# Attention with one ring of four PSUM places, one copy per turned tile and a written order on three engines

## The chip, the cores and the metric

The kernel runs on one core of one Trainium2 chip. The metric is the time of one execution on the device in microseconds (us); of several executions the median counts. A core has TensorE (PE in the profile, with its weight loads as PEld), VectorE (DVE), ScalarE (ACT), GpSimd (POOL) and SyncE (SP), which here issues the DMAs. SBUF is the working memory, PSUM the eight banks that TensorE writes its products to.

## The reference

An attention with a learned bias, then two expert layers; only the attention is touched:

```python
scores = scale * np.matmul(q, k.transpose(0, 1, 3, 2))      # 4 batches, 8 heads, 576 x 64
rel = (pos[:, None] - pos[None, :]).astype(np.float32)
x = (np.log1p(np.abs(rel)) / psi_i)[..., None]
bias = np.maximum(x @ w1 + b1, 0.0) @ w2                     # one 576 x 576 table a head
scores = scores + bias.transpose(2, 0, 1)[None, :, :, :]
scores = scores - np.max(scores, axis=-1, keepdims=True)
attn = np.exp(scores)
attn = attn / (np.sum(attn, axis=-1, keepdims=True) + 1e-09)
out = np.matmul(attn, v)                                     # then moe, then moe2, on 2304 x 512
```

## The kernel before

The bias tables are made first. Then come 16 **pairs** `i` of two heads of one batch, each in nine **tiles** `t` of 128 queries (tile t = 6 takes the last 64 queries of both heads). The expert layers follow; their first weights and inputs are prepared inside the last pairs by hooks.

A tile passes through these steps; the letter is the one that the change gives it:

- **S** (`scores`, L366): six matmuls into a PSUM tile `s` of two banks (twelve for t = 6). q and k are each split into a high and a low part (`split`, L339 and L341 on POOL, four instructions a pair).
- **z** (L376, DVE): bias minus scores and the row's minimum, read from PSUM.
- **e** (L387, ACT): the exponential, with the row's sum.
- **T** (`transposes`, L405): ten transpositions of e into two PSUM tiles `t` of one bank.
- **g** (L414 on ACT for one of them, L416 on DVE for the other): copies of 320 elements a partition into SBUF, the operand of the product with v.

A pair has besides: **P** (`pv`, L429), the product with v in two halves (256 and 320 queries, 20 records each in the trace), issued in two chunks of 12 and 8 records with a score and a transposition between them; **O** (L436), its copy `xo` and the DMA of it to the scratch `xT` (L438); **R** (`sums`, L444 and L445), the inverse of the sums; **Q** (L447, L449), the inverses transposed, copied and stored to `rs`.

PSUM is held by three pools: `a_ps_s` 2 x 2 banks, `a_ps_t` 3 x 1, `a_ps_o` 1: all eight banks. Scores run `LA` = 4 tiles ahead of the transpositions. From pair 1 on the instructions of PE keep the order in which the program issues them (`pin`); on the other engines the scheduler sets the order. SP loads `raw` (q and k of a pair), `v` and, for every fourth pair, the bias rows `nb` two pairs ahead.

Around the last pairs the hooks of the expert layer run on DVE and ACT: `x_sum` (L538) scales the attention's output as it is read back, `w_narrow` (L565, L568, L569) unpacks a weight, `w_split` (L588) makes its high part, `up` (L601) is the first product, with L612 behind it.

Of the kernel before, what the change touches and what calls it, by code (L numbers as in the profile page):

```python
# [68 lines left out]
def bias_phase(tc, ident, W, cpack, lcol, prow, xmain, xtail, att):  # L69
# [3 lines left out]
    with ExitStack() as ctx:  # L73
# [159 lines left out]
        for k in range(1, NG):  # L233
            nc.sync.dma_start(xm_t[:, k], xmain[:, k])
        att.load(0)
        for k in range(NG):
            cs = [c for c in range(3, -1, -1) if k <= NG - 1 - c]
            if k < 5:
                cs.append(4)
            done = 0  # L240
            for n_, c in enumerate(cs):
                unit(k, c)
                if c in (2, 3) and k + c == 8:
                    att.bias_first(3 - c)
# [14 lines left out]
class Attention:  # L259
# [57 lines left out]
    def load(self, i):  # L317
        nc = self.nc
        hp, b = self.pairs[i]
        if b == 0 and hp > 0:  # L320
            self.bias_tile(hp)
            self.bias_rows(hp, 0, 4)
            self.bias_rows(hp, 4, 1)
        raw = self.rp.tile([P, 1792], F32, tag="raw", name=f"raw{i}")
        nc.sync.dma_start(raw, self.qk[hp, b])
        v = self.vp.tile([P, 2, 5, D], F32, tag="v", name=f"v{i}")
        nc.sync.dma_start(v, self.v_l[hp, b])
        self.st[i] = dict(hp=hp, b=b, i=i, raw=raw, v=v)

    def split(self, i, k):  # L330

# [16 lines left out]
    def scores(self, i, t):  # L348
        nc, st = self.nc, self.st[i]
        slot = self.SLOT[t]  # L350
        if slot == 0:
            st["sum"] = self.op.tile([P, 9], F32, tag="sum", name=f"sum{i}")
        s = self.ps_s.tile([P, 2, 512], F32, tag="s", name=f"s{i}_{t}")
        if slot < 4:
            terms = [(P * slot, 0)]
        elif slot == 4:
            terms = [(512, 0), (576, 1)]
        else:
            terms = [(704 + P * (slot - 5), 1)]
# [14 lines left out]
        z = self.zp.tile([P, S], F32, tag="z", name=f"z{i}_{t}")
        m = self.zp.tile([P, 1], F32, tag="m", name=f"m{i}_{t}")
        nc.vector.tensor_tensor_reduce(  # L376
            out=z.rearrange("p (a b) -> p a b", a=2),
            in0=s[:, :, :288],
            in1=self.nb[st["hp"]][:, slot].rearrange("p (a b) -> p a b", a=2),
            scale=-0.125,  # L380
            scalar=3.0e38,
            op0=ALU.add,
            op1=ALU.min,
            accum_out=m,
        )
        e = self.zp.tile([P, S], F32, tag="e", name=f"e{i}_{t}")
        nc.scalar.activation(e, z, AF.Exp, bias=m, scale=-1.0, accum_out=st["sum"][:, slot : slot + 1])  # L387
        st["e", t] = e

    def g_tile(self, st, h, half):  # L390
        if ("g", h, half) not in st:
            st["g", h, half] = self.gp.tile([P, 5, 320], F32, tag="g", name=f"g{st['i']}_{h}_{half}")
        return st["g", h, half]

    def transposes(self, i, t):

        nc, st = self.nc, self.st[i]
        slot = self.SLOT[t]
        e = st.pop(("e", t))
        tp = [self.ps_t.tile([P, 5, 64], F32, tag="t", name=f"t{i}_{t}_{r}") for r in range(2)]  # L400
        for c in range(5):
            for r in range(2):
                q = slice(64 * r, 64 * r + 64)
                k0 = min(P * c, S - P)
                self.pin(i, nc.tensor.transpose(tp[r][:, c], e[q, k0 : k0 + P], self.ident[q, q]))  # L405
        for r in range(2):
            if slot == 4:
                dst = self.g_tile(st, r, 1)[:, :, 256:]
            else:
                n = slot % 5  # L410
                c0 = P * (n % 2) + 64 * r
                dst = self.g_tile(st, slot // 5, n // 2)[:, :, c0 : c0 + 64]
            if r == 0:
                nc.scalar.activation(dst, tp[r], AF.Copy)  # L414
            else:
                nc.vector.tensor_copy(dst, tp[r])  # L416

    def pv(self, i, half, chunks):
        nc, st = self.nc, self.st[i]
        n = 320 if half else 256  # L420
        if chunks[0] == 0:
            st["o"] = self.ps_o.tile([P, 320], F32, tag="o", name=f"o{i}_{half}")
        o = st["o"]
        for c in chunks:
            for h in range(2):
                g = st["g", h, half]
                self.pin(
                    i,
                    nc.tensor.matmul(  # L429
                        o[64 * h : 64 * h + 64, :n], st["v"][:, h, c], g[:, c, :n], start=c == 0, stop=c == 4  # L430
                    ),
                )
        if chunks[-1] < 4:
            return
        xo = self.op.tile([P, 320], F32, tag="xo", name=f"xo{i}_{half}")
        nc.vector.tensor_copy(xo[:, :n], o[:, :n])  # L436
        c0 = st["b"] * S + 256 * half
        nc.sync.dma_start(self.xT[st["hp"], :, c0 : c0 + n], xo[:, :n])  # L438

    def sums(self, i):  # L440
        nc, st = self.nc, self.st[i]
        hp, c0 = st["hp"], st["b"] * S
        r = self.op.tile([P, 9], F32, tag="r", name=f"r{i}")
# [11 lines left out]
    def open(self, ctx):  # L455
        tc = self.tc
        self.zp = ctx.enter_context(tc.tile_pool(name="a_z", bufs=LA + 1, reuse_waits="tile"))
        self.op = ctx.enter_context(tc.tile_pool(name="a_out", bufs=2, reuse_waits="tile"))
        self.gp = ctx.enter_context(tc.tile_pool(name="a_g", bufs=4, reuse_waits="tile"))
        self.ps_s = ctx.enter_context(tc.tile_pool(name="a_ps_s", bufs=2, space=PSUM, reuse_waits="tile"))  # L460
        self.ps_t = ctx.enter_context(tc.tile_pool(name="a_ps_t", bufs=3, space=PSUM, reuse_waits="tile"))
        self.ps_o = ctx.enter_context(tc.tile_pool(name="a_ps_o", bufs=1, space=PSUM, reuse_waits="tile"))
        self.open_set(ctx, 1)

    def run(self, hooks):
        np_ = len(self.pairs)
        steps = [(i, t) for i in range(np_) for t in range(9)]
        pend = []
        for k in range(4):
            self.split(1, k)  # L470
        for i, t in steps[:LA]:
            self.scores(i, t)
        for n, (i, t) in enumerate(steps + [(np_, 0)]):
            if n + LA < len(steps):
                self.scores(*steps[n + LA])
            if i < np_:
                self.transposes(i, t)
            if n:
                i1, t1 = steps[n - 1]
                if t1 == 8:  # L480
                    self.sums(i1)
            if pend:
                pend.pop(0)()
            if n and t1 in self.DONE:
                pend += [lambda i=i1, half=self.DONE[t1], c=c: self.pv(i, half, c) for c in ((0, 1, 2), (3, 4))]
            if t < 4 and 0 < i < np_ - 1:
                self.split(i + 1, t)
            if t == 2 and i + 2 < np_:
                self.load(i + 2)
            for f in hooks.get((i, t), ()):  # L490
                f()
        for f in pend:
            f()


class Moe:
# [734 lines left out]
```

## Time and profile before

| | us |
|---|---|
| runs | 899.84, 907.18, 911.56 |
| median | 907.18 |
| profiled execution, span of the trace | 898.7 |
| its mean granted TensorE clock | 0.953 |
| PE busy in it | 813.7 (91%) |
| DVE busy in it | 604.0 (67%) |
| ACT busy in it | 487.1 (54%) |
| the pairs, from the first z to the end of the last product | 85.9 to 375.3 |

The profile gives the profiled execution's span, 898.7 us, and no other time for it; the median lies 8.5 us above, and the runs lie 11.7 us apart. Busy shares are averages over stages with different limits, so the rows are read by pair: pair `i` is the time from its first z to that of the next pair.

### The profile page before, as it was taken

How to read it: one execution, taken by the hardware profiler on the slowest of the kernel's cores; microseconds unless marked ns; L12 is line 12 of the kernel's file. 1: busy time of each engine (PE TensorE's matmuls, PEld its weight loads, DVE VectorE, ACT ScalarE, POOL GpSimd, SP SyncE). 2: the span in 40 equal slices, each digit the busy share in tenths (PEclk: the TensorE clock that was granted, in tenths of full speed). 3: DMA queues.
4: the chain of work that ended last, by engine and by line, in shares of the span. 5: the costliest groups of instructions: out<-in, count | busy, mean ns of one | idle time of the engine just before them, and what ended most of it. 6: DMA issues, size and time to landing. Idle time of an engine off the chain costs nothing.

```text
span 898.7 us, 18451 instructions
## 1 busy us (share of the span) xinstructions
PE 813.7 (91%) x7428; PEld 655.7 (73%) x7428; DVE 604.0 (67%) x1085; ACT 487.1 (54%) x1019; POOL 288.7 (32%) x205
## 2 busy tenths in 40 slices
PE   5876999899998799799999999999998999998894
PEld 5876766666666566489899988988897889987342
DVE  8865678788688678899943755585666567565203
ACT  8643566666566566344444665665655656555002
POOL 7954225243243221421432143134243223131000
PEclk9987699999999889899999999999998999999997
DMA  6798853834735311566500110040000004336995
GB/s 197 223 201 185 200 162 116 218 92 123 192 92 184 108 51 67 189 205 216 180 3 1 36 36 1 1 170 19 1 18 9 1 1 163 119 96 208 394 399 216
DMA packets 59493, 114.44 MB, mean 127 GB/s; under 512 B 10640, under 2 KB 38160, under 8 KB 57360
## 3 DMA queue, kind: packets, MB, share of 16 engines
q1 hardware_dynamic: 59408, 113.26, 41.5%
q8 instruction: 58, 0.95, 0.4%
q14 instruction: 27, 0.22, 0.1%
HBM read 91.95 MB, written 21.29 MB: 126 GB/s over the span
## 4 chain that ended last, share of the span: by engine, by line
PE 60%; DVE 19%; DMA 9%; ACT 4%; issue 4%; POOL 1%; SPq 1%; DVEq 0%; ACTq 0%; POOLq 0%
PE ys L633 17%; PE h L601 16%; PE o L429 6%; PE acc L160 5%; DVE z L376 4%; PE s L366 4%; DMA xT<-xo 3%; PE ops L1005 2%; PE t L405 2%; DVE r L444 2%; PE hps L1005 2%; DVE g L416 2%; DMA stage<-in_w_dram 2%; DMA W<-rows 1%; ACT e L387 1%
## 5 line engine op out<-in xcount | busy, mean ns | idle before, releaser
L612 DVE SCALAR_TENSOR_TENSOR g<-g,nal 128x384 f32<-128x384 f32 x96 | 90.7, 945 | 78.6 <-ACT g L611 78.3
L376 DVE CUSTOM_DVE_ANT_0 z<-s,nb 128x576 f32<-128x576 f32 x144 | 107.2, 746 | 43.1 <-PE s L366 32.1
L387 ACT ACTIVATE e<-z,m 128x576 f32<-128x576 f32 x144 | 111.2, 772 | 45.0 <-DVE m L376 43.4
L405 PE MATMUL t<-ident,e 64*128 64x64 f32 x1440 | 92.5, 235 | 24.2 <-ACT g L414 19.3
L619 ACT ACTIVATE gr<-g 128x384 fp32r<-128x384 f32 x95 | 49.8, 524 | 103.4 <-DVE g L612 103.2
L405 PEld LDWEIGHTS t<-ident,e 64*128 64x128 f32 x1440 | 76.2, 144 | 39.8 <-ACT g L414 32.8
L429 PE MATMUL o<-g,v 128*64 128x256 f32 (+1 forms) x640 | 100.4, 437 | 0.3 <-DVE g L416 0.3
L414 ACT ACTIVATE g<-t 128x320 f32<-128x320 f32 x144 | 60.9, 426 | 52.4 <-PE t L405 52.4
L160 PE MATMUL acc<-wp,mask 128*128 128x64 bf16 (+1 forms) x1680 | 59.7, 202 | 18.2 <-issue 10.9
L366 PE MATMUL s<-kh,qh 64*128 64x288 f32 x320 | 66.2, 394 | 10.3 <-DVE rows L185 6.6
L621 DVE TENSOR_TENSOR gr<-g,gr 128x384 fp32r<-128x384 f32 x79 | 53.9, 682 | 32.2 <-ACT gr L619 31.1
L160 PEld LDWEIGHTS <-mask 128*128 128x128 bf16 (+1 forms) x1680 | 58.1, 106 | 19.7 <-issue 12.9
L339 POOL TENSOR_SCALAR qh<-raw 128x1216 fp32r<-128x1216 f32 x16 | 19.5, 1218 | 161.3 <-PE s L366 157.7
L416 DVE COPY g<-t 128x320 f32<-128x320 f32 x144 | 69.4, 483 | 2.7 <-PE t L405 2.5
L609 ACT ACTIVATE g<-h 128x384 f32<-128x384 f32 x96 | 46.7, 486 | 44.8 <-PE h L601 44.3
L366 PEld LDWEIGHTS s<-kh,qh 64*128 64x128 f32 x320 | 34.5, 197 | 41.2 <-issue 21.5
L429 PEld LDWEIGHTS o<-g,v 128*64 128x64 f32 x640 | 43.4, 144 | 28.2 <-issue 5.3
L141 ACT ACTIVATE mask<-pr,wb 128x576 bf16<-128x576 f16 (+4 forms) x81 | 46.9, 664 | 21.6 <-PE acc L160 21.6
L366 PE MATMUL s<-kl,qh 64*128 64x288 f32 x320 | 51.8, 306 | 0.0
L366 PE MATMUL s<-kh,ql 64*128 64x288 f32 x320 | 51.5, 305 | 0.0
L621 POOL TENSOR_TENSOR gr<-g,gr 128x384 fp32r<-128x384 f32 x16 | 22.6, 1416 | 85.9 <-ACT gr L619 85.9
L611 ACT ACTIVATE g<-h 128x384 f32<-128x384 f32 x96 | 46.5, 485 | 0.0
(1004 smaller groups left out, 2059.8 us busy)
## 6 DMA issues: line engine op xcount, KB each, us to landing
stage<-in_w_dram SPq DMA_DIRECT2D x16, 1024.0 KB
ep<-in_mw_dram SPq DMA_DIRECT2D x30, 512.0 KB
raw<-in_qk_dram SPq DMA_DIRECT2D x16, 896.0 KB
nb<-W SPq DMA_DIRECT2D x12, 576.0 KB
v<-in_v_l_dram SPq DMA_DIRECT2D x16, 320.0 KB
pre<-in_mw_dram SPq DMA_DIRECT2D x10, 512.0 KB
er<-in_mw_dram SPq DMA_DIRECT2D x9, 512.0 KB
em<-in_mw_dram SPq DMA_DIRECT2D x8, 512.0 KB
```

The lines of the kernel that those rows point to most:

```text
L160: nc.tensor.matmul(dst[:, u // 8, :, :, 4 * (u % 8) : 4 * (u % 8) + 4], mask[:, (16 * k + u) % RING, cols], wp[:, part], start=part == 0, ...
L366: nc.tensor.matmul(s[:, hf, :288], st["q", a][d, o : o + P], st["k", b][d, 288 * h : 288 * h + 288], start=n_ == 0, stop=n_ == len(seq) - 1,),
L376: nc.vector.tensor_tensor_reduce(out=z.rearrange("p (a b) -> p a b", a=2), in0=s[:, :, :288], in1=self.nb[st["hp"]][:, slot].rearrange("p ...
L387: nc.scalar.activation(e, z, AF.Exp, bias=m, scale=-1.0, accum_out=st["sum"][:, slot : slot + 1])
L405: self.pin(i, nc.tensor.transpose(tp[r][:, c], e[q, k0 : k0 + P], self.ident[q, q]))
L414: nc.scalar.activation(dst, tp[r], AF.Copy)
L416: nc.vector.tensor_copy(dst, tp[r])
L429: nc.tensor.matmul(o[64 * h : 64 * h + 64, :n], st["v"][:, h, c], g[:, c, :n], start=c == 0, stop=c == 4),
L601: nc.tensor.matmul(h, w_[:, c * P : (c + 1) * P], x_[:, c], start=c == 0 and n_ == 0, stop=c == NC - 1 and n_ == 2,)
L612: nc.vector.scalar_tensor_tensor(g, neg, self.nal[:, f : f + 1], g, ALU.mult, ALU.add)
L621: eng.tensor_tensor(gl, g, gh.bitcast(F32), ALU.subtract)
L633: i = self.nc.tensor.matmul(self.ys[blk][t], g_[:, t * P : (t + 1) * P], w_[:, 512:], start=f == 0 and n_ == 0, stop=f == NF - 1 and n_ == 2,)
```

## The change

All products of the attention go to **one ring** of four PSUM places of two banks (`a_ps`): scores, transposed tiles and output products in the order of their issue. A transposed tile takes one place and is copied by one instruction of 640 elements, on DVE for t = 1, 2 and 5, on ACT otherwise. The output product of a half is one burst of 20 records. The transposed inverses go to the second bank of half 1's place. `LA` is 5. The order within a pair is written out (`ROUND`; + is the next pair, - the one before), and DVE and ACT are pinned to it as PE is. The splits and the loads move: `raw` after T0, `v` after T4, the four splits of pair i+2 after T5 to T8 of pair i (before: of pair i+1 after T0 to T3). The inverse is made with another instruction, (sum + 1e-9) max sum.

```diff
-LA = 4
+LA = 5
...
-    DONE = {3: 0, 8: 1}
+    TURN_DVE = (1, 2, 5)
+    ROUND = tuple(
+        (w[0], int(w[1]), {"": 0, "+": 1, "-": -1}[w[2:]])
+        for w in (
+            "T0 z5 S6 g0 e3 T1 z6 S7 T2 e4 g1 P1- g2 e5 z7 e6 e7 S8 O1- T3 Q1- S0+ z8 g3 T4 g4 z0+ S1+ T5 e8 z1+ S2+ "
+            "T6 e0+ g5 P0 z2+ g6 e1+ R0 S3+ O0 e2+ T7 z3+ S4+ g7 T8 z4+ S5+ g8"
+        ).split()
+    )
...
-        s = self.ps_s.tile([P, 2, 512], F32, tag="s", name=f"s{i}_{t}")
+        s = self.ps.tile([P, 2, 512], F32, tag="p", name=f"s{i}_{t}")
...
-        tp = [self.ps_t.tile([P, 5, 64], F32, tag="t", name=f"t{i}_{t}_{r}") for r in range(2)]
+        tp = self.ps.tile([P, 2, 512], F32, tag="p", name=f"t{i}_{t}")
...
-            if r == 0:
-                nc.scalar.activation(dst, tp[r], AF.Copy)
-            else:
-                nc.vector.tensor_copy(dst, tp[r])
+    def gather(self, i, t):
...
+        if t in self.TURN_DVE:
+            self.pin(i, nc.vector.tensor_copy(dst, src))
+        else:
+            self.pin(i, nc.scalar.activation(dst, src, AF.Copy))
...
-    def pv(self, i, half, chunks):
+    def pv(self, i, half):
...
+        op = self.ps.tile([P, 2, 512], F32, tag="p", name=f"o{i}_{half}")
...
+        for c in range(5):
             for h in range(2):
...
+                        op[64 * h : 64 * h + 64, 0, :n], st["v"][:, h, c], g[:, h, c], start=c == 0, stop=c == 4
...
+        if half:
+            self.pin(i, nc.tensor.transpose(op[:9, 1, :P], st["r"], self.ident))
+
+    def put(self, i, half):
...
+        self.pin(i, nc.vector.tensor_copy(xo[:, :n], st["o", half][:, 0, :n]))
...
+    def inverse(self, i):
...
-        nc.vector.tensor_scalar(r, st["sum"], 1e-9, None, ALU.add)
-        nc.vector.reciprocal(r, r)
-        tp = self.ps_t.tile([P, P], F32, tag="t", name=f"tr{i}")
+        self.pin(i, nc.vector.scalar_tensor_tensor(r, st["sum"], 1e-9, st["sum"], ALU.add, ALU.max))
+        self.pin(i, nc.vector.reciprocal(r, r))
+
+    def put_sums(self, i):
...
-        self.gp = ctx.enter_context(tc.tile_pool(name="a_g", bufs=4, reuse_waits="tile"))
-        self.ps_s = ctx.enter_context(tc.tile_pool(name="a_ps_s", bufs=2, space=PSUM, reuse_waits="tile"))
-        self.ps_t = ctx.enter_context(tc.tile_pool(name="a_ps_t", bufs=3, space=PSUM, reuse_waits="tile"))
-        self.ps_o = ctx.enter_context(tc.tile_pool(name="a_ps_o", bufs=1, space=PSUM, reuse_waits="tile"))
+        self.gp = ctx.enter_context(tc.tile_pool(name="a_g", bufs=1, reuse_waits="tile"))
+        self.ps = ctx.enter_context(tc.tile_pool(name="a_ps", bufs=4, space=PSUM, reuse_waits="tile"))
...
+        for i in range(-1, np_ + 1):
+            for what, t, di in self.ROUND:
...
+                if t == 0 and i + 2 < np_:
+                    self.load(i + 2)
+                if t == 4 and i + 2 < np_:
+                    self.load_v(i + 2)
+                if 5 <= t and i + 2 < np_:
+                    self.split(i + 2, t - 5)
```

In the order of the instructions, a name has its pair and tile (`s7_6` is the score of pair 7, t = 6) and a running number. On **PE**, at the end of pair 6's product in pair 7's round, before:

```order
L429 MATMUL o6_1_4428<-g6_1_1_4265,v6_3585 64x320
L366 MATMUL s7_6_4436<-kh7_4172,qh7_4095 128x288 x2
L366 MATMUL s7_6_4436<-kl7_4173,qh7_4095 128x288 x2
L366 MATMUL s7_6_4436<-kh7_4172,ql7_4096 128x288 x2
...
L405 MATMUL t7_2_0_4454<-ident_63,e7_2_4318 128x64
L429 MATMUL o6_1_4428<-g6_0_1_4237,v6_3585 64x320
L366 MATMUL s7_7_4482<-kh7_4172,qh7_4095 128x288 x2
```

and after:

```order
L379 MATMUL s7_7_4281<-kh7_3915,ql7_3843 128x288 x2
L437 MATMUL t7_2_4288<-ident_63,e7_2_4184 128x64 x10
L465 MATMUL o6_1_4302<-g6_1_4101,v6_3542 64x320 x10
L470 MATMUL o6_1_4302<-ident_63,r6_4171 9x128
L379 MATMUL s7_8_4324<-kh7_3915,qh7_3842 128x288 x2
L379 MATMUL s7_8_4324<-kl7_3916,qh7_3842 128x288 x2
L379 MATMUL s7_8_4324<-kh7_3915,ql7_3843 128x288 x2
L437 MATMUL t7_3_4334<-ident_63,e7_3_4265 128x64 x10
```

The product is one run of ten matmuls, between the transposition of tile 2 and the score of tile 8, and the transposition of the sums stands right behind it.

On **DVE**, around the inverse of pair 6's sums (`r6`), before:

```order
L376 ISA z7_0_4248,m7_0_4249<-s7_0_4241,nb1_2984 128x576
L376 ISA m7_0_4249 128x1
L444 TENSOR_SCALAR r6_4387<-sum6_3937 128x9
L416 COPY g6_1_1_4265<-t6_5_1_4254 128x5x64
L445 RECIPROCAL r6_4387<-r6_4387 128x9
L376 ISA z7_1_4282,m7_1_4283<-s7_1_4275,nb1_2984 128x576
L376 ISA m7_1_4283 128x1
L416 COPY g6_1_1_4265<-t6_6_1_4288 128x5x64
L436 COPY xo6_0_4305<-o6_0_4268 128x256
```

and after:

```order
L451 COPY g6_1_4101<-t6_5_4113 128x2x5x64
L397 ISA z7_2_4165,m7_2_4166<-s7_2_4132,nb1_2856 128x576
L397 ISA m7_2_4166 128x1
L483 SCALAR_TENSOR_TENSOR r6_4171<-sum6_3794 128x9
L484 RECIPROCAL r6_4171<-r6_4171 128x9
L476 COPY xo6_0_4181<-o6_0_4154 128x256
L397 ISA z7_3_4200,m7_3_4201<-s7_3_4174,nb1_2856 128x576
L397 ISA m7_3_4201 128x1
```

The inverse stands two z later, behind z7_2 and right ahead of the copy of the first half's output; the copies of tiles 6 to 8 are gone from DVE.

On **DVE** in the last round, around the output of pair 14 (`xo14_1`, `rt14`), after:

```order
L397 ISA z15_7_6550,m15_7_6551<-s15_7_6514,nb3_5070 128x576
L605 TENSOR_SCALAR wr2_6621<-stage_5632 128x1024
L608 SCALAR_TENSOR_TENSOR wr2_6621<-stage_5632,wr2_6621 128x1024
L476 COPY xo14_1_6564<-o14_1_6535 128x320
L605 TENSOR_SCALAR wr1_6578<-stage_5632 128x1024
L609 SCALAR_TENSOR_TENSOR wr2_6621<-stage_5632,wr2_6621 128x1024
L608 SCALAR_TENSOR_TENSOR wr1_6578<-stage_5632,wr1_6578 128x1024
L578 TENSOR_TENSOR xa3_0_8079<-xa3_0_8079,rb3_0_8080 128x384
L609 SCALAR_TENSOR_TENSOR wr1_6578<-stage_5632,wr1_6578 128x1024
L490 COPY rt14_6587<-o14_1_6535 9x128
L397 ISA z15_8_6593,m15_8_6594<-s15_8_6557,nb3_5070 128x576
```

Two weights are unpacked (`wr2`, `wr1`) between z15_7 and z15_8, and the place of `o14_1` is read for the last time behind them.

## Rows read from the trace of the kernel before

**Rows 1.** Windows by pair: us, busy PE, PEld, DVE, ACT, POOL, clock, DMA, GB/s.

```profile
85.89:104.78 18.89, 16.77 (x134) 13.72 (x134) 10.93 (x25) 8.98 (x23) 4.76 (x4) 0.52 0.82 198
...
232.34:250.67 18.33, 16.32 (x195) 11.41 (x196) 13.41 (x34) 10.69 (x28) 5.97 (x5) 0.91 0.54 174
...
250.67:266.59 15.92, 14.73 (x193) 10.46 (x195) 13.33 (x34) 10.72 (x28) 5.97 (x5) 1.00 0.34 98
282.50:306.69 24.19, 16.83 (x202) 11.64 (x204) 18.05 (x40) 12.28 (x32) 10.63 (x7) 0.91 0.59 203
...
322.85:342.77 19.92, 17.69 (x193) 12.47 (x195) 15.16 (x35) 11.20 (x29) 4.38 (x3) 0.83 0.11 33
...
342.77:375.28 32.51, 28.80 (x282) 18.58 (x283) 28.79 (x57) 16.98 (x39) 6.48 (x4) 0.90 0.37 134
```

**Rows 2.** Timeline of PE in pair 10: start, us, line, operation, count.

```profile
251.00 1.52 PE L429 MATMUL o<-g,v 128*64 128x256 f32 x12
252.45 0.40 PE L366 MATMUL s<-kh,qh 64*128 64x288 f32 x2
...
258.05 0.28 PE L447 MATMUL tr<-ident,r 128*9 128x128 f32 x1
...
259.32 1.84 PE L429 MATMUL o<-g,v 128*64 128x320 f32 x12
261.08 0.40 PE L366 MATMUL s<-kh,qh 64*128 64x288 f32 x2
...
261.98 0.47 PE L405 MATMUL t<-ident,e 64*128 64x64 f32 x10
262.38 1.30 PE L429 MATMUL o<-g,v 128*64 128x320 f32 x8
263.61 0.40 PE L366 MATMUL s<-kh,qh 64*128 64x288 f32 x2
...
264.11 0.47 PE L405 MATMUL t<-ident,e 64*128 64x64 f32 x10
264.39 0.38 PE L366 MATMUL s<-kh,qh 64*128 64x288 f32 x2
```

**Rows 3.** Waits in pairs 3 and 4: total us, times, longest.

```profile
PEld t L405 <- ACT g L414: 4.6, 9, 0.6
```

**Rows 4.** Timeline of DVE in pair 10; idle time before it in brackets.

```profile
251.34 2.38 DVE L444 TENSOR_SCALAR r<-sum 128x9 f32<-128x9 f32 x1
...
264.43 0.76 DVE L376 CUSTOM_DVE_ANT_0 z<-s,nb 128x576 f32<-128x576 f32 x1 [0.21 <-PE s L366]
```

**Rows 5.** Timeline of POOL in pair 10.

```profile
249.08 1.22 POOL L339 TENSOR_SCALAR qh<-raw 128x1216 fp32r<-128x1216 f32 x1 [12.36 <-PE s L366]
...
250.90 2.79 POOL L341 TENSOR_TENSOR ql<-raw,qh 128x1216 fp32r<-128x1216 f32 x1
```

**Rows 6.** One line's instructions, L444 and L612: ns shortest/median/longest, starts.

```profile
L444 DVE TENSOR_SCALAR r<-sum x16: 161/2370/2393, 102.4 to 363.7; 128x9 f32<-128x9 f32 x16
...
L612 DVE SCALAR_TENSOR_TENSOR g<-g,nal x96: 590/619/2739, 370.0 to 816.1; 128x384 f32<-128x384 f32 x96
```

**Rows 7.** Groups of ACT and DVE by shape: count, busy us, mean ns.

```profile
L387 ACT ACTIVATE e<-z,m 128x576 f32<-128x576 f32 x144 | 111.2, 772 | 45.0 <-DVE m L376 43.4 <-DVE r L444 0.4
...
L672 ACT ACTIVATE yh<-ys 128x512 fp32r<-128x512 f32 x15 | 8.2, 595 | 3.4 <-PE ys L633 3.4
...
L416 DVE COPY g<-t 128x320 f32<-128x320 f32 x144 | 69.4, 483 | 2.7 <-PE t L405 2.5
...
L1034 DVE COPY emo<-o 128x512 f32<-128x512 f32 x7 | 4.4, 685 | 0.3 <-PE o L1032 0.3
```

**Rows 8.** Timeline of ACT in pair 10: a copy of a turned tile.

```profile
264.62 0.44 ACT L414 ACTIVATE g<-t 128x320 f32<-128x320 f32 x1 [0.65 <-PE t L405]
```

**Rows 9.** Timeline of DVE: an output copy of pair 8, a hook's product in pair 12.

```profile
237.92 0.43 DVE L436 COPY xo<-o 128x256 f32<-128x256 f32 x1 [1.00 <-DMA xT<-xo]
...
302.72 2.10 DVE L538 TENSOR_TENSOR stage<-stage 128x384 f32<-128x384 f32 x1 [2.12 <-DMA stage<-xT]
```

More of the change, by code (lines that the diff above doesn't have):

```diff
@@ L325, in load, with load_v @@
         nc.sync.dma_start(raw, self.qk[hp, b])
[L326 to L328 removed]
+        self.st[i] = dict(hp=hp, b=b, i=i, raw=raw)
+    def load_v(self, i):
+        st = self.st[i]
+        st["v"] = self.vp.tile([P, 2, 5, D], F32, tag="v", name=f"v{i}")
+        self.nc.sync.dma_start(st["v"], self.v_l[st["hp"], st["b"]])
     def split(self, i, k):
@@ L373, in scores, with least, power, g_tile @@
                 )
+        st["s", t] = s
+    def least(self, i, t):
+        st = self.st[i]
+        slot = self.SLOT[t]
+        s = st.pop(("s", t))
         z = self.zp.tile([P, S], F32, tag="z", name=f"z{i}_{t}")
         m = self.zp.tile([P, 1], F32, tag="m", name=f"m{i}_{t}")
[L376 to L384, printed above, removed]
-        )
+        self.pin(
+            i,
+            self.nc.vector.tensor_tensor_reduce(
+                out=z.rearrange("p (a b) -> p a b", a=2),
+                in0=s[:, :, :288],
+                in1=self.nb[st["hp"]][:, slot].rearrange("p (a b) -> p a b", a=2),
+                scale=-0.125,
+                scalar=3.0e38,
+                op0=ALU.add,
+                op1=ALU.min,
+                accum_out=m,
+            ),
+        )
+        st["z", t] = z, m
+    def power(self, i, t):
+        st = self.st[i]
+        slot = self.SLOT[t]
+        z, m = st.pop(("z", t))
         e = self.zp.tile([P, S], F32, tag="e", name=f"e{i}_{t}")
-        nc.scalar.activation(e, z, AF.Exp, bias=m, scale=-1.0, accum_out=st["sum"][:, slot : slot + 1])
+        self.pin(
+            i,
+            self.nc.scalar.activation(e, z, AF.Exp, bias=m, scale=-1.0, accum_out=st["sum"][:, slot : slot + 1]),
+        )
         st["e", t] = e
[L390 to L393, printed above, removed]
+    def g_tile(self, st, half):
+        if ("g", half) not in st:
+            n = 320 if half else 256
+            st["g", half] = self.gp.tile([P, 2, 5, n], F32, tag=f"g{half}", name=f"g{st['i']}_{half}")
+        return st["g", half]
     def transposes(self, i, t):
@@ L466, in run @@
         np_ = len(self.pairs)
-        steps = [(i, t) for i in range(np_) for t in range(9)]
-        pend = []
+        act = dict(S=self.scores, z=self.least, e=self.power, T=self.transposes, g=self.gather)
         for k in range(4):
             self.split(1, k)
[L471 to L493, printed above, removed]
+        for i in range(-1, np_ + 1):
+            for what, t, di in self.ROUND:
+                j = i + di
+                if not 0 <= j < np_:
+                    continue
+                if what in act:
+                    act[what](j, t)
+                elif what == "P":
+                    self.pv(j, t)
+                elif what == "O":
+                    self.put(j, t)
+                elif what == "R":
+                    self.inverse(j)
+                else:
+                    self.put_sums(j)
+                if what != "T":
+                    continue
+                if t == 0 and i + 2 < np_:
[4 more added lines that the diff above has]
+                    self.split(i + 2, t - 5)
+                for f in hooks.get((i, t), ()):
+                    f()
 class Moe:
```

41 lines of the change are left out of this document (20 added, 21 removed).

## The prediction

> **What bounds the kernel now.** I read the windows by pair first. In a steady pair PE is busy for 14.73 of 15.92 us, DVE for 13.33, ACT for 10.72 (pair 10, from 250.67) [rows 1]; so PE is the bound, but with over a microsecond of holes and DVE close behind it. The timeline of PE gives what each step costs it, as the distance from one start to the next [rows 2]: a score .50 (263.61 to 264.11), the double score of tile 6 .90, a transposition .28 ahead of a score (264.11 to 264.39) and .40 ahead of a product (261.98 to 262.38), the first 12 records of a product 1.45 (256 queries) and 1.76 (320), the last 8 of the larger 1.23, so .13 a record; the same slope by width makes that .106 for 256 queries and 1.02 for its last 8. The transposed sums cost at most .28. Before, a pair is 8 x .50 + .90 + 4 x .40 + 5 x .28 + 1.45 + 1.02 + 1.76 + 1.23 + .28 = 13.64. The waits say what fills the rest: PE's weight loads wait for ACT's copy of a turned tile, 4.6 us in two pairs [rows 3], 2.3 a pair. 13.64 + 2.3 = 15.9, the pair as measured. The wait is a chain through the three one-bank places of the turned tiles: while the scores and transpositions run without a product between them, DVE needs a z and a copy for each tile (.76 + .48 by their durations [rows 4, 7], less their overlap some 1.08), ACT an e and a copy (.77 + .43 [rows 7, 8]), and PE only .78. PE is ahead there, and waits for the place.
>
> **The change part by part, for a steady pair.**
>
> *PE.* Two transpositions ahead of a product fall away (2 x .12), and each burst pays its entry once: 1.45 + 8 x .106 = 2.30 and 1.76 + 8 x .13 = 2.80 [rows 2]. The sum is 8 x .50 + .90 + 7 x .28 + 2 x .40 + 2.30 + 2.80 + .28 = 13.04 us. That is the floor.
>
> *DVE.* Nine copies of 320 elements go (9 x .48 = 4.35) and three of 640 come. No row shows a copy of 640; it lies between one of 512 (.685, L1034) and two of 320 (.97), and by the slope between 320 and 512 it takes .82 [rows 7]. DVE is busy for 13.33 - 4.35 + 2.46 = 11.4 us, if the inverse keeps its length. So DVE comes off the bound.
>
> *ACT.* Nine copies of .43 go, six come at .71 (between .595 for 512 and twice .43, by the same slope) [rows 7, 8]: 10.72 - 3.85 + 4.26 = 11.1 us, below PE.
>
> *The ring.* A score's place is held from its first matmul to the end of its z: 263.61 to 264.43 + .76 = 265.19, 1.58 us [rows 2, 4]. A turned tile's is held from 264.11 to the end of ACT's copy, which began at 264.62 [rows 8] and will take .71: 1.22 us. Four places shared by the two kinds pass a tile every (1.58 + 1.22) / 4 = .70 us, just under PE's .78. A burst adds slack, since it holds one place for over 2 us while DVE and ACT catch up. Between .70 and .78 little is left, so I add .35 for places that come free late, once or twice a pair: **13.4 us**. The bounds: 13.04 with no wait, and 15.9 if the old wait comes back under the new name (rival C).
>
> *The inverse.* Its first instruction takes 2.38 us for nine elements, and ends at 253.72; POOL's ql runs from 250.90 to 253.69 [rows 4, 5]. Of 16 it took 161 ns in the quickest and 2370 in the median [rows 6]: it stands behind POOL's instruction. The new form reads the sums twice, both times from SBUF. The nearest rows to it are those of L612, the same kind of instruction: 619 ns in the median and 2739 in the longest [rows 6], so that form too can be held up, and I don't count the 2.2 us as saved. The Trainium skill, "SBUF — State Buffer", § Who interferes with whom, has the rule: an instruction of VectorE with two inputs in SBUF contends with one of GpSimd that reads SBUF, as one in a 2-port mode does, so by it the new form frees nothing; with a form that is free, a pair with no cover would gain those 2.2 us. What changes is the place. POOL's qh waits for the last score that reads the pair's q, as now, and ql starts 1.8 us behind it and lasts 2.8 [rows 5]; with qh some .8 behind S8's start, ql spans 2.6 to 5.4. On PE S8 is followed by T3, S0, T4, S1, T5, S2, T6 and P0: z2 ends and R stands at about 4.2, P0 ends at 3 x .78 + .50 + .40 + 2.30 = 5.5. R thus waits some 1.2 us under P0, and what is queued behind it on DVE is first the copy of P0's product, which isn't there sooner. Cost: 0 to .2, inside the .35. Without this cover, z3 and the next score would be late by some 1.0.
>
> *Loads, stores, splits.* The splits wait for the same score as before and are issued earlier, so no score waits for them. Raw's load now stands ahead of both of a round's stores of xT in SP's queue, and v's stands behind one. The stores matter: `xo` has two buffers, and DVE waited 1.00 us for the store from two copies ago [rows 9]. That pair took 18.33 at a clock of 0.91 [rows 1]. Shorter pairs give that store less time, so I leave these 2.4 us, and bound the case from 3 us gained to 4.5 lost, in three places.
>
> *The pairs that are not steady* [rows 1]. Pair 0 runs at a clock of 0.52 beside loads (DMA share 0.82): nothing. Pairs 1 to 11 and 13: 12 x (15.92 - 13.4) = 30. Pair 12 takes 24.19, since DVE, in its order, waits for the attention's output to be read back (2.12 us, and 2.10 for the product itself [rows 9]); those waits stay, and are longer if the pair gets there sooner, while DVE's 18.05 us lose 1.9: 3.5, between 0 and 8. Pair 14 takes 19.92 at a clock of 0.83; fewer holes would win back half of what the clock took: 3.5, between 2.5 and 6. Pair 15 is DVE's (28.79 of 32.51) with the weights' unpacking; there the inverse was not held up, the first expert product no longer runs inside the attention but behind the last product, and two unpackings stand between z15_7 and z15_8 with a ring place held: I take 0, between 4 lost and 3 gained.
>
> Sum: 30 + 3.5 + 3.5 = 37 us. Against the profiled execution 898.7 - 37 = 861.7; the median lies 8.5 above it, so 907.2 - 37 = **870 us**. Its own range, with .35 a pair either way (4) and the bounds above in part, is 858 to 883.
>
> **The rivals.** *B: half the gain.* The .70 a tile holds only if a copy starts as soon as its tile is there. ACT does in order what is written: if each copy stands behind an e (.77 [rows 7]), a tile's holding is 1.58 + 1.22 + .77 = 3.57, a quarter of it .89, and nine tiles lose 9 x .11 = 1.0; the pair is 14.4. A held-up inverse without its cover costs the same 1.0. For it: e and copies alternate in the written order. Against it: most of these collisions fall into the bursts. 12 x 1.5 = 18, and 6 elsewhere: 24, so 883.
>
> *C: the wait has only changed its name.* If also each z stands behind a copy of .82 on DVE, the holding is 4.3, 1.08 a tile: 9 x .30 = 2.7 more than 13.04, so 15.75, nothing gained. This needs every tile to collide on both engines; but DVE has three copies a pair, not nine. With the last pair's bounds 905.
>
> *D: slower, by PE's clock.* After holes in PE the rows show the lower level of the clock (1.2 in place of 2.4 GHz) for a part of the time: a mean of 0.91 in pair 9, 0.83 in pair 14, which takes 4.0 us more than a steady one [rows 1]. With all products through one ring a late copy stops scores, transpositions and products alike, where now each has places of its own; if that drops the clock in every pair, for a share f of PE's work, a pair takes up to 13.2 x (1 + f). It is even at f = .2, 2% slower from f = .30; at .35, 17.8 us, 14 x 1.9 = 27 more: 934. Against it: steady pairs hold 1.00 with 2.3 us of waits, and the change shortens them. The Trainium skill, "TensorE: Matmul & The Clock Gate", § A second HAM failure mode: psum-queue depth-cycling, tells of a kernel whose short idle times from cycling through PSUM banks made the clock swing; by that rule D would come, but the steady pairs, which cycle through banks too, show 1.00 throughout.
>
> **How the numbers follow.** A .66 (870), B .20 (883), C .09 (905), D .05 (934). The likeliest gives the time. A measurement of this kernel tells about 2% from no change: faster is below 889, slower above 925. A and most of B are faster: .80. The rest of B and C are within: .14. D and the worst ends of the last pairs: .06. The range takes in A and B with their bounds, 853 to 892, and leaves out C and D and some of A's ends, 2 in 10.
>
> **What would show it.** The pair's period 13.2 to 13.6 with PE busy for nearly all of it, the wait for ACT's copy under .5 us a pair, the clock 1.00; DVE at 9 to 11.5 us and ACT at 11 a pair; the inverse still 1 us or more wherever POOL runs ql, and no hole in PE behind it. Wrong would be: scores that wait for z or copies in each tile (B, C), clocks below 0.95 in steady pairs (D), xT's stores waited for in more pairs than every fourth, or a last pair longer than 36 us.

## The result and the profile after

The changed kernel takes **882.18 us** (median of four runs, 880.18 to 887.10) against 907.13 for the kernel before (four runs): a ratio of 0.974, with a 95% interval of 0.969 to 0.979. It is faster by 25 us, inside the range, at two thirds of the forecast gain. The profiled execution took 880.18 us with a span of 878.4, 20.3 below the span of before.

The windows by pair of the changed kernel, in the columns of [rows 1]; pairs 5, 9, 10, 12, 14, 15 and the start of the expert layer:

```profile
158.46:176.16 17.70, 14.93 (x197) 11.78 (x193) 10.70 (x27) 11.04 (x25) 5.97 (x5) 0.90 0.61 185
215.17:230.89 15.72, 13.44 (x197) 10.31 (x193) 10.70 (x28) 11.06 (x25) 6.01 (x5) 1.00 0.67 205
230.89:243.92 13.03, 13.03 (x197) 10.27 (x193) 10.87 (x28) 11.05 (x25) 6.01 (x5) 1.00 0.40 124
256.94:279.81 22.87, 15.23 (x195) 11.64 (x193) 15.96 (x29) 11.88 (x27) 11.48 (x8) 0.86 0.61 216
...
294.53:312.45 17.92, 15.16 (x199) 11.80 (x195) 11.72 (x28) 11.23 (x26) 5.02 (x4) 0.90 0.19 59
312.45:344.30 31.85, 22.64 (x273) 15.56 (x270) 24.82 (x45) 16.21 (x33) 4.74 (x2) 0.89 0.39 132
344.30:360.00 15.70, 10.61 (x44) 8.80 (x43) 12.92 (x15) 5.18 (x10) 7.05 (x7) 0.78 0.76 230
```

A steady pair takes 13.03 us and PE is busy for all of it: the floor of 13.04 that was summed from PE's pitches. Eight pairs (2 to 4, 6 to 8, 10, 11) take 13.00 to 13.04. Pairs 5 and 9 don't, and the last pair is as long as before.

The waits of the changed kernel in two steady pairs (132.4 to 158.46), which answer to [rows 3]:

```profile
POOL qh L352 <- PE s L379: 21.1, 3, 7.0
ACT g L453 <- PE t L437: 4.1, 5, 1.1
DVE xo L476 <- PE o L470: 2.2, 2, 1.1
DVE z L397 <- PE s L379: 1.3, 4, 0.5
PEld o L470 <- issue: 1.0, 2, 0.5
PEld s L379 <- DVE r L484: 0.8, 2, 0.4
```

No matmul of PE waits any more, and no weight load for a copy; now ACT and DVE wait for PE.

The copies of 640 elements, by shape, which answer to [rows 7]:

```profile
L451 DVE COPY g<-t 128x640 f32<-128x640 f32 x48 | 38.2, 819 | 1.4 <-PE t L437 1.4
```

```profile
L453 ACT ACTIVATE g<-t 128x640 f32<-128x640 f32 x96 | 67.0, 702 | 43.0 <-PE t L437 39.8
```

.82 and .70 us: the estimates were .82 and .71.

The inverse in pair 3's window of the changed kernel, and the burst above it: timelines of POOL, DVE and PE, as in [rows 2, 4, 5].

```profile
133.26 2.80 POOL L354 TENSOR_TENSOR ql<-raw,qh 128x1216 fp32r<-128x1216 f32 x1
```

```profile
135.37 0.72 DVE L483 SCALAR_TENSOR_TENSOR r<-sum 128x9 f32<-128x9 f32 x1
...
136.56 0.42 DVE L476 COPY xo<-o 128x256 f32<-128x256 f32 x1 [0.22 <-PE o L465]
```

```profile
134.13 2.38 PE L465 MATMUL o<-g,v 128*64 128x256 f32 x20
...
140.80 2.91 PE L465 MATMUL o<-g,v 128*64 128x320 f32 x20
```

The new form ends at 136.09, .03 behind ql: it is held up as the old one was, but only for the .7 us that ql still has to run, and the copy behind it waits for the product anyway.

Where the gain was lost: at the start of pair 1, PE (second line) waits behind the inverse of pair 0 on DVE (first line). The order of pair 0 is not pinned, and its inverse stands beside ql (100.76 to 103.52 on POOL):

```profile
100.94 2.60 DVE L483 SCALAR_TENSOR_TENSOR r<-sum 128x9 f32<-128x9 f32 x1 [0.94 <-ACT e L417]
```

```profile
104.47 0.40 PE L379 MATMUL s<-kh,qh 64*128 64x288 f32 x2 [2.12 <-DVE m L397]
```

An output copy in pair 5 on DVE waits for the store of the copy two back, and PE behind it,

```profile
166.05 0.42 DVE L476 COPY xo<-o 128x256 f32<-128x256 f32 x1 [3.67 <-DMA xT<-xo]
```

```profile
166.54 0.52 PE L437 MATMUL t<-ident,e 64*128 64x64 f32 x10 [2.62 <-DVE xo L476]
```

in pair 12 PE waits for the copy of pair 11's transposed sums, which stands behind two instructions of a hook on DVE,

```profile
279.36 0.80 PE L437 MATMUL t<-ident,e 64*128 64x64 f32 x10 [5.21 <-DVE rt L490]
```

and in the last pair and behind it PE waits for the copy of pair 14's transposed sums, then for the expert layer's input:

```profile
334.33 1.47 PE L437 MATMUL t<-ident,e 64*128 64x64 f32 x20 [6.28 <-DVE rt L490]
...
352.38 0.69 PE L641 MATMUL h<-x,w0h 128*128 128x384 f32 x1 [3.91 <-ACT x L583]
354.06 0.69 PE L641 MATMUL h<-x,w0h 128*128 128x384 f32 x1 [0.99 <-DVE x L584]
```

The account between the two profiled executions, from the first z of pair 0 on: the first z is .6 later; pair 0 gains 1.7, the eight steady pairs 23.1, pairs 1, 5, 9 and 13 together 2.9, pair 12 1.3, pair 14 2.0: the last pair begins at 312.45 in place of 342.77, 30.3 earlier. From there to the end it is 878.4 - 312.45 = 566.0 us in place of 898.7 - 342.77 = 555.9. **Ten of thirty microseconds are given back behind the start of the last pair.** Both figures are of one execution each.

### The profile page after: what moved, and what is told of

Read it like the earlier page. It is cut to its first block, busy times and chain, and to the rows that moved or that the text cites. A ratio compares the mean times of both kernels' runs of the same rounds, so it can differ in the third digit from the quotient of the medians.

```text
span 878.4 us, 18352 instructions
## 1 busy us (share of the span) xinstructions
PE 785.1 (89%) x7428; PEld 651.2 (74%) x7428; DVE 562.3 (64%) x989; ACT 492.0 (56%) x971; POOL 286.4 (33%) x205
## 4 chain that ended last, share of the span: by engine, by line
PE 42%; DVE 4%; ACT 2%; DMA 2%; issue 1%; POOL 0%; SPq 0%; DVEq 0%; ACTq 0%
PE ys L673 17%; PE h L641 16%; PE ops L1045 3%; PE hps L1045 2%; DMA rb<-rs 2%; PE lp L732 1%; DVE xa L578 1%; DVE g L652 1%; PE turn L1054 0%; DVE gr L661 0%; PE tl L779 0%; DVE emo L1074 0%; ACT g L649 0%; PE sp L791 0%; PE sp L792 0%
## 5 line engine op out<-in xcount | busy, mean ns | idle before, releaser
L652 DVE SCALAR_TENSOR_TENSOR g<-g,nal 128x384 f32<-128x384 f32 x96 | 87.7, 913 | 82.6 <-ACT g L651 82.3
L437 PE MATMUL t<-ident,e 64*128 64x64 f32 x1440 | 72.5, 232 | 24.8 <-DVE rt L490 11.5
L453 ACT ACTIVATE g<-t 128x640 f32<-128x640 f32 x96 | 67.0, 702 | 43.0 <-PE t L437 39.8
L437 PEld LDWEIGHTS t<-ident,e 64*128 64x128 f32 x1440 | 69.2, 147 | 28.2 <-issue 16.6
L465 PE MATMUL o<-g,v 128*64 128x256 f32 (+1 forms) x640 | 88.6, 423 | 0.5 <-ACT g L453 0.5
L379 PE MATMUL s<-kh,qh 64*128 64x288 f32 x320 | 64.2, 396 | 13.6 <-DVE rows L185 6.7
L354 POOL TENSOR_TENSOR ql<-raw,qh 128x1216 fp32r<-128x1216 f32 x16 | 44.7, 2792 | 0.0
```

The lines of the kernel that those rows point to most:

```text
L379: nc.tensor.matmul(s[:, hf, :288], st["q", a][d, o : o + P], st["k", b][d, 288 * h : 288 * h + 288], start=n_ == 0, stop=n_ == len(seq) - 1,),
L437: self.pin(i, nc.tensor.transpose(tp[:, r, 64 * c : 64 * c + 64], e[q, k0 : k0 + P], self.ident[q, q]))
L453: self.pin(i, nc.scalar.activation(dst, src, AF.Copy))
L465: nc.tensor.matmul(op[64 * h : 64 * h + 64, 0, :n], st["v"][:, h, c], g[:, h, c], start=c == 0, stop=c == 4),
L652: nc.vector.scalar_tensor_tensor(g, neg, self.nal[:, f : f + 1], g, ALU.mult, ALU.add)
```

## The experiments

Three theories for the 2.9 us of a steady pair. P: products can take any free place. C: one copy a tile takes work off DVE. O: the written order on DVE and ACT. The table holds one steady pair (pair 7, from its first z to that of the next) from the windows of each run.

| kernel | pair 7, us | PE busy | DVE busy | clock |
|---|---|---|---|---|
| before | 15.90 | 14.75 | 13.31 | 1.00 |
| changed | 13.00 | 13.00 | 10.86 | 1.00 |
| e1 own places, one copy | 17.05 | 14.41 | 10.49 | 1.00 |
| e2 ring, two copies | 14.39 | 13.78 | 11.69 | 1.00 |
| e3 old places, two copies, written order | 16.05 | 14.52 | 12.65 | 1.00 |
| e4 changed, DVE and ACT not pinned | 17.79 | 14.86 | 12.78 | 0.90 |
| e5 changed, products in two chunks | 14.34 | 14.12 | 9.77 | 1.00 |
| e6 changed, inverse early | 17.18 | 14.41 | 11.98 | 0.90 |
| e9 before, inverse in one step | 15.51 | 14.75 | 11.31 | 1.00 |
| e10 as e6, inverse in one step | 13.98 | 13.10 | 10.12 | 1.00 |
| e11 as e4, inverse in one step | 13.86 | 13.44 | 10.12 | 1.00 |

**Own places (e1).**

```diff
-        s = self.ps.tile([P, 2, 512], F32, tag="p", name=f"s{i}_{t}")
+        s = self.ps.tile([P, 2, 512], F32, tag="s", name=f"s{i}_{t}")
...
-        tp = self.ps.tile([P, 2, 512], F32, tag="p", name=f"t{i}_{t}")
+        tp = self.ps.tile([P, 2, 512], F32, tag="t", name=f"t{i}_{t}", bufs=1)
...
-        op = self.ps.tile([P, 2, 512], F32, tag="p", name=f"o{i}_{half}")
+        op = self.ps.tile([P, 2, 512], F32, tag="o", name=f"o{i}_{half}", bufs=1)
...
-        self.ps = ctx.enter_context(tc.tile_pool(name="a_ps", bufs=4, space=PSUM, reuse_waits="tile"))
+        self.ps = ctx.enter_context(tc.tile_pool(name="a_ps", bufs=2, space=PSUM, reuse_waits="tile"))
```

> The changed kernel, with the ring undone and all else kept: scores have two places of two banks of their own, turned tiles one, output products one. In the changed kernel a steady pair takes 13.02 us and PE waits for nothing in it. Theory P (places): what removed the 2.3 us of waits a pair is that any product can take any free place. Then a turned tile, whose place is held some 1.2 us from its first transposition to the end of its copy, stops the next one outside the bursts: about .4 us lost for seven of nine tiles, a pair of 15 to 16.5 us, with PE waiting for the copies of turned tiles. Theory C (copies): it was the one copy a tile in place of two, which takes 1.9 us a pair off DVE; places don't matter: 13.0 to 13.4. Theory O (order): it was the written order on DVE and ACT: 13.0 to 13.4 too.

It took 927.32 us, and pair 7 17.05. The waits in that pair:

```profile
PEld t L437 <- ACT g L453: 2.6, 5, 0.6
...
PEld t L437 <- DVE g L451: 1.6, 2, 0.9
```

PE's weight loads wait for the one place of the turned tiles seven times a pair, 4.2 us. Theory P's wait came, larger than its 15 to 16.5 us allowed; C and O fall as sole causes. One copy a tile with this division of the places is worse than before, but before's own division, with one and a half places for turned tiles, was not run with one copy.

**Two copies in the ring (e2).**

```diff
-        if t in self.TURN_DVE:
-            self.pin(i, nc.vector.tensor_copy(dst, src))
-        else:
-            self.pin(i, nc.scalar.activation(dst, src, AF.Copy))
+        halves = [(dst[:, r], src[:, r]) for r in range(2)]
+        self.pin(i, nc.scalar.activation(*halves[0], AF.Copy))
+        self.pin(i, nc.vector.tensor_copy(*halves[1]))
```

> The changed kernel with the ring, but each turned tile copied by two instructions of 320 elements, one on ACT and one on DVE, as before. Theory P: the ring suffices; DVE's work rises to some 12.8 us and ACT's falls by .4, both still under PE's 13.0, so a pair of 13.0 to 13.8. Theory C: the wait comes back: 15 us or more. Theory O: 13.0 to 13.4.

892.73 us, 14.39 a pair: between the theories. The ring with two copies, the bursts and the written order is 1.5 below before; one copy brings the other 1.4.

**Old places, written order (e3)**, with the copies of e2, the bursts and the early scores kept:

```diff
...
+        s = self.ps.tile([P, 2, 512], F32, tag="s", name=f"s{i}_{t}", bufs=2)
...
+        tp = [self.ps.tile([P, 5, 64], F32, tag="t", name=f"t{i}_{t}_{r}", bufs=3) for r in range(2)]
...
+        op = self.ps.tile([P, 320], F32, tag="o", name=f"o{i}_{half}", bufs=1)
...
```

> The changed kernel with the PSUM places and the copies of before (scores two places of two banks, half turned tiles three of one bank, output one, the transposed sums in a turned tile's place; two copies a tile), but in the written order, with whole output bursts and scores five tiles ahead. Theory O: the order is what counts, 13.0 to 13.6 a pair. Theories P and C: three one-bank places for half tiles give one and a half tiles, so PE waits for copies again: 15 to 16 us a pair.

918.64 us, 16.05 a pair, with PE's weight loads waiting 1.9 us of it for ACT's copies and .6 for DVE's. The order and the bursts without the ring bring nothing; the ring is worth 1.7 with two copies (e2 against this run) and one copy adds 1.4 only in the ring.

**The order left to the scheduler (e4)**: DVE and ACT not pinned.

```diff
-    def pin(self, i, ins):
-        if i > 0:
+    def pin(self, i, ins, free=False):
+        if i > 0 and not free:
...
```

(with True at each call of DVE and ACT.)

> The changed kernel with DVE and ACT not pinned in the attention: the scheduler sets their order, PE keeps the written one. Its order has the inverse of the sums two z earlier, and copies and z exchanged in places. Theory O: the gain goes at least by half, 14.5 us a pair or more. Theories P and C: 13.0 to 13.5; the inverse, started earlier in POOL's ql, takes 1 to 2.4 us on DVE.

917.65 us, 17.79 in pair 7 at a clock of 0.90, worse than before. In its timelines the inverse stands .08 behind the start of ql and lasts until its end, and the product of half 0 waits for the z behind it:

```profile
210.53 2.71 DVE L485 SCALAR_TENSOR_TENSOR r<-sum 128x9 f32<-128x9 f32 x1 [0.17 <-ACT e L418]
```

```profile
210.45 2.76 POOL L354 TENSOR_TENSOR ql<-raw,qh 128x1216 fp32r<-128x1216 f32 x1
```

```profile
214.16 3.73 PE L467 MATMUL o<-g,v 128*64 128x256 f32 x20 [2.50 <-DVE m L397]
```

The burst then takes 3.73 us in place of 2.38; the mean granted clock in its window (214.16 to 217.90) is 0.63, so it runs in part at the lower level. Theory O was right on the size but its cause might be one instruction; e6, e10 and e11 test that.

**Products in two chunks (e5).**

```diff
-            "T0 z5 S6 g0 e3 T1 z6 S7 T2 e4 g1 P1- g2 e5 z7 e6 e7 S8 O1- T3 Q1- S0+ z8 g3 T4 g4 z0+ S1+ T5 e8 z1+ S2+ "
-            "T6 e0+ g5 P0 z2+ g6 e1+ R0 S3+ O0 e2+ T7 z3+ S4+ g7 T8 z4+ S5+ g8"
+            "T0 z5 S6 g0 e3 T1 z6 S7 T2 e4 g1 P1- g2 e5 z7 e6 e7 S8 T3 p1- O1- Q1- S0+ z8 g3 T4 g4 z0+ S1+ T5 e8 z1+ S2+ "
+            "T6 e0+ g5 P0 z2+ g6 e1+ R0 S3+ T7 p0 O0 e2+ z3+ S4+ g7 T8 z4+ S5+ g8"
...
```

(P is the first chunk there, p the second; `pv` takes the chunk's part of the product.)

> The changed kernel with each output product in two chunks of 12 and 8 records again, with a score and a transposition between them; the ring, the single copies and the written order stay. By PE's pitches two more transpositions ahead of a product and two more entries cost some .5 us: 13.5 a pair if PE is all that counts. If the burst matters for the ring (it holds one place while the others come free), a place is held over 1 us longer, PE waits: 14 us or more.

A pair takes 14.34: the burst is worth 1.3 us in the ring, not the .5 of its pitches. Of the 1.3, 1.1 shows as PE busy longer and .2 as waits, so the number is that of the second case but its waits did not come; what the .6 of busy time above the pitches is stays open. The one execution took 878.87 us all the same (before on its chip 901.26): pairs 5 and 9 were 3.7 us shorter than in the changed kernel, and the stretch from the start of the last pair to the end was 877.1 - 319.1 = 558.0, 8 shorter. So the whole time says nothing of the burst.

**The inverse early (e6)**, two z ahead of its place, where the scheduler had it in e4:

```diff
-            "T0 z5 S6 g0 e3 T1 z6 S7 T2 e4 g1 P1- g2 e5 z7 e6 e7 S8 O1- T3 Q1- S0+ z8 g3 T4 g4 z0+ S1+ T5 e8 z1+ S2+ "
-            "T6 e0+ g5 P0 z2+ g6 e1+ R0 S3+ O0 e2+ T7 z3+ S4+ g7 T8 z4+ S5+ g8"
+            "T0 z5 S6 g0 e3 T1 z6 S7 T2 e4 g1 P1- g2 e5 z7 e6 e7 S8 O1- T3 Q1- S0+ z8 g3 T4 g4 z0+ S1+ T5 e8 R0 z1+ S2+ "
+            "T6 e0+ g5 P0 z2+ g6 e1+ S3+ O0 e2+ T7 z3+ S4+ g7 T8 z4+ S5+ g8"
```

> The changed kernel with one thing moved: the inverse of the sums two z earlier in DVE's written order (right behind z0 of the next pair), where the scheduler put it in the kernel with the free order (18.1 us a pair). It will start as POOL's ql begins and end with it, some 2.7 us later. The product of half 0 then waits for its place in the ring, which z1 frees: if DVE's stall is passed on, 15.5 to 16 us a pair with PE waiting 2.5 us for a z; that would explain half of what the free order lost. If the burst and DVE's slack cover it, 13.0 to 14.0, and the free order's loss lies in the other exchanges.

916.88 us, 17.18 in pair 7 at a clock of 0.90. On DVE (first line) the inverse waits .98 us for the exponential of tile 8 and takes 1.91, not the 2.7 expected, since ql is under way by then; behind the z that follows, PE starts the burst late (second line):

```profile
206.79 1.91 DVE L483 SCALAR_TENSOR_TENSOR r<-sum 128x9 f32<-128x9 f32 x1 [0.98 <-ACT e L417]
```

```profile
209.62 3.69 PE L465 MATMUL o<-g,v 128*64 128x256 f32 x20 [2.77 <-DVE m L397]
```

One instruction of nine elements, moved by two places, costs 4.2 us a pair: 2.8 of PE's wait, and the rest by the clock behind it. The burst takes 3.69 us in place of 2.38, and the granted clock in its window (209.62 to 213.31) is 0.63, against 1.00 ahead of the wait and behind the burst. That is most of what e4 lost.

**The inverse in one step (e9, e10, e11).** The reciprocal reads the sums themselves; the 1e-9 is not added. In before (e9):

```diff
-        nc.vector.tensor_scalar(r, st["sum"], 1e-9, None, ALU.add)
-        nc.vector.reciprocal(r, r)
+        nc.vector.reciprocal(r, st["sum"])
```

> The kernel before, with the first of the inverse's two instructions left out: the reciprocal reads the sums themselves, so the 1e-9 is not added. In before that instruction took 2.38 us of DVE in each steady pair, held up by POOL's ql, and the reciprocal was never lengthened. Theory P (places): PE's waits come from the three places of the turned tiles, the pair stays at 15.4 us or more. Theory R (the inverse): DVE, 2.2 us late in each pair, is what makes the copies late behind it; the pair falls by 1 us or more, to 14.0 to 14.8.

The inverse now takes 210 ns, DVE is busy 2.0 us less, and the pair only .4 shorter (15.51; 903.47 us). PE's weight loads still wait 2.2 us for ACT's copies:

```profile
PEld t L405 <- ACT g L414: 2.2, 5, 0.6
```

So before was bound by the places: theory P.

> The changed kernel with the inverse early, as in the run with 17.5 us a pair, but by one reciprocal that reads the sums themselves (the 1e-9 is not added). If the loss there was DVE held up by POOL's ql, and the lower clock behind PE's wait, the pair is back at 13.0 to 13.4 with a clock of 1.00. If the place in the order is to blame (the wait for the exponential of tile 8, the ring), it stays above 14.5.

879.97 us, 13.98 at a clock of 1.00: the stall behind ql, with the clock that it takes down, is 3.2 of the 4.2 us; 1.0 stays with the place, since DVE still waits .98 us for the exponential of tile 8 there, and PE .9 for the z behind.

> The changed kernel with DVE and ACT not pinned (18.1 us a pair), and the inverse by one reciprocal that reads the sums themselves (the 1e-9 is not added). If the written order does nothing but keep the inverse out of POOL's ql, 13.0 to 13.4 a pair. If the written order of z and copies counts beside it, 14 us or more.

877.65 us, 13.86: of the 4.8 us that the free order lost, 3.9 were the inverse. The written order of z and copies is worth .9 beside it.

**Four buffers for xo (e7).**

```diff
-        xo = self.op.tile([P, 320], F32, tag="xo", name=f"xo{i}_{half}")
+        xo = self.op.tile([P, 320], F32, tag="xo", name=f"xo{i}_{half}", bufs=4)
```

> The changed kernel with four buffers for the output copy xo in place of two. In the changed kernel DVE waited 3.67 and 3.15 us in pairs 5 and 9 for the store of the copy two back, which lay behind bias rows in the DMA queues; those pairs took 17.70 and 15.72 in place of 13.02. If the buffers are the cause, both take 13.0 to 13.3, 7 us in all, and the time falls by 5 to 8 us, to about 875. If the end of the kernel waits for weights that come when they come, the pairs gain and the time does not: 880 to 882.

Pairs 5 and 9 take 13.02 and 13.01 us, as the windows of this run show (the third line is the last pair):

```profile
155.64:168.66 13.02, 13.02 (x197) 10.27 (x193) 10.85 (x28) 11.04 (x25) 5.98 (x5) 1.00 0.83 253
207.71:220.72 13.01, 13.01 (x197) 10.25 (x193) 10.84 (x26) 11.03 (x25) 5.97 (x5) 1.00 0.83 252
297.55:331.50 33.95, 24.36 (x272) 16.17 (x268) 25.59 (x45) 16.20 (x33) 6.14 (x7) 0.85 0.40 126
```

872.61 us, ratio to before 0.970 (0.964 to 0.975), where the changed kernel has 0.974: a gain that the intervals don't separate. The last pair begins 14.9 us earlier than in the changed kernel, and the span is 10.0 shorter, so five more are given back behind it. The pairs did what was expected; the time fell by 4 us by the ratios, below the 5 to 8.

**The unpacking later (e8).**

```diff
-PIN = 2
+PIN = 3
...
-NARROW = ((-1, 0), (-1, 3), (-1, 5))
-WSPLIT = ((-1, 0), (-1, 3))
+NARROW = ((-1, 0), (-1, 4), (-1, 5))
+WSPLIT = ((-1, 0), (-1, 4))
```

> The changed kernel with the unpacking of the weights 1 and 2 moved behind the copy of the transposed sums of pair 14 in DVE's order (their hooks two places later). In the changed kernel PE waited 6.28 us in the last pair for that copy, since the last reader of its ring place stood behind them. If that wait is a loss, the last pair takes 26 to 28 us in place of 31.9, and the time falls by 3 to 6 us. If the first expert product, which needs the same weights, is late instead, the time stays within 2 us.

870.97 us, ratio 0.966 (0.961 to 0.971). (`PIN` is the number of weights whose unpacking keeps its written place on DVE, so the edit moves one hook and pins one more.) The 6.28 us wait for `rt` is gone, but the last pair is not shorter, at a clock of 0.80:

```profile
315.30:349.30 34.00, 26.60 (x272) 16.85 (x268) 26.55 (x45) 16.32 (x33) 5.46 (x3) 0.80 0.41 130
```

PE waits 2.7 us for ACT's copies and 2.1 for the inverse instead, and 2.4 for a z as in the changed kernel. The gain lies behind it: from the last product to the end it is 870.8 - 349.3 = 521.5 us, in the changed kernel 878.4 - 344.3 = 534.1. The time fell by 7 us by the ratios, more than the 3 to 6 expected, and elsewhere than expected; the two intervals (0.961 to 0.971, 0.969 to 0.979) just overlap.

**Both (e12).**

> The changed kernel with both: four buffers for xo and the unpacking of two weights behind the copy of the transposed sums. If the two losses are separate, their gains add: 4 and 7 us below the changed kernel by their ratios to before, so a ratio of .961 to before, some 866 to 872 us. If both only move the same wait for weights and for the read-back output at the start of the expert layer, no better than the better of the two: .966.

**860.54 us**, ratio 0.956 (0.953 to 0.959) to a before of 900.85 on the same chip: better than both kernels and than either edit alone, with intervals apart. The gain is more than the sum that was expected (.961), so the losses are separate. The last pair still takes 32.78 us, but from its start to the end it is now 851.4 - 296.0 = 555.4 us (e8: 870.8 - 315.3 = 555.5), as before's 555.9. The profiled execution is the fastest of this kernel's four, 7.3 us below their median, so the ratios of e7 and e12 (0.970 and 0.956, with the unpackings' place as the only difference) carry more than this stretch.

## Why the prediction held, point by point

**What bounds before** was right. The sum by pitches said that PE waits 2.3 us a pair for places of turned tiles; e9 took 2.0 us off DVE and the waits stayed, e3 kept the places and the waits stayed.

**The steady pair** was better than forecast: 13.0, not 13.4. The .35 for places that come free late is not there; the places' .70 a tile against PE's .78 was enough. The likeliest case A was the mechanism. That the total landed on the number of rival B, 883, is chance: no steady pair lost 1.0 to late places. **C** and **D** did not come in the changed kernel, whose steady pairs hold a clock of 1.00. D's mechanism is real, though: in e4 and e6 one stall a pair takes the clock to 0.90 and the kernel past before. The Trainium skill, "TensorE: Matmul & The Clock Gate", § A second HAM failure mode: psum-queue depth-cycling, tells of short idle times from cycling through PSUM banks that made the clock swing. This case's traces agree in part: the clock fell behind one wait of 2.5 to 2.8 us for a place, while neither the ring by itself nor before's waits of at most .6 us took it down.

**The inverse** was right in its place and wrong in its price. It is held up until ql's end under the burst and costs nothing, as forecast, but it takes .72 us (.718 in the median of 16), where 1 us or more was named as a sign. By the Trainium skill, "SBUF — State Buffer", § Who interferes with whom, a VectorE instruction with two inputs in SBUF contends with one of GpSimd that reads SBUF. The traces agree: the new form is held up (.72 beside ql, .16 without, and 2.71 in e4). Without cover it was said to cost 1.0. In e6, where it takes 1.91 us, the pair loses 4.2: 3.2 by the stall, which the ring passes to PE and which takes the clock down, and 1.0 by the place (e10). The same loss stood in the changed kernel unnoticed: pair 0 is not pinned, its inverse takes 2.60 us beside ql, and pair 1 takes 15.67 us (14.12 in e10, with the reciprocal alone).

**The step that failed: the last pair, "I take 0, between 4 lost and 3 gained"**, and what follows it. Measured: 10 lost from the start of the last pair to the end, in one execution of each kernel. Its own length stayed (31.85 to the end of the last product; before 342.77 to 374.75, 31.98), but before ran the first expert products inside it, from 360.3 on, and the changed kernel starts them at 344.1, behind the last product. Then PE waits 3.9 and 1.0 us for an input behind DVE's unpacking, at a clock of 0.78 in that window. The bounds were set for the pair alone; its cover for the expert layer's start was not counted. In e8 and e12, with two unpackings elsewhere, the stretch is 555.5 and 555.4 us; in e7, with the buffers alone, it is 868.4 - 297.6 = 570.8. The eight profiled ring kernels that keep the unpackings' hooks lie between 558.0 (e5) and 572.0 (e10), and e9, the old kernel but for its inverse, has 562.2. So the place of the unpackings, which the prediction had named and priced at nothing, is a cause, worth 1.4% of the time between e7 and e12; single executions don't settle the size of the 10. The edit also lets the scheduler order the expert layer anew, and how much is the wait itself and how much that order stays open.

**The smaller terms.** Pairs 5 and 9 lose 4.7 and 2.7 us against a steady pair to xo's buffers. Before, they already stood .6 and 2.4 above one, so 4.4 are new, just inside the bound of 4.5 ("in three places"; two came). Pair 1 gained nothing in place of 2.5, since pair 0's inverse has no cover. Steady pairs brought 23 for eight where 20 were forecast, so the twelve pairs summed as 30 brought 26.0. Pairs 12 and 14 gained 1.3 and 2.0 in place of 3.5 each, their hooks' waits staying as said; in pair 12 PE waits 5.2 us for the transposed sums' copy behind a hook's two, the wait of the last pair again. In the other runs pair 12 took 17.7 to 27.0 us, so a size for it from one execution is worth little.

**The base.** The medians lie 25 apart, the spans 20: the span before lay 8.4 below the median of its runs, after 3.8. The forecast of 861.7 for the profiled execution was missed by 16.7, that of the median by 12. The 5 us between them are luck of the base: with the spans' gain the median would have been 887, still inside the range, but above the 858 to 883 of the sum's own range.

## What to carry to other kernels

Here a pool of places shared by products of different lives was worth more than the two divisions of the same banks that were run, with each product's release following the order of issue; the test beforehand is holding time over places against the engine's pitch, here .70 against .78. In this ring one late instruction stopped what stood behind it on three engines, so look for the instruction whose length depends on another engine and put it under a burst, in the first pair too. When steady stages get shorter, look at what runs at their edges: buffers sized for the old period, and a tail that was covered by them.

## What the runs showed of the hardware

A VectorE instruction of nine elements took 0.16 us alone and up to 2.71 us beside GpSimd's ql, ending .03 us behind it, in the scalar form and in the form with two inputs; the reciprocal with one input took 210 ns beside the same ql (e9, e10). With one wait of PE of 2.5 to 2.8 us in pair 7 its mean granted clock was 0.90 (e4, e6), with the fall in the burst behind the wait, while before's waits of at most .6 us, 2.3 us a pair in all, left it at 1.00.
